# An attention and mixture-of-experts kernel: input loads three chunks ahead instead of four, the first chunks in halves, and three groups of small VectorE work in another order

## The chip, the cores and the metric

The kernel runs on one NeuronCore of a Trainium2 chip. The metric is the time of one execution on the device in microseconds (us), median of several runs.

## The reference

A linear attention with decay runs over 4 batches, 8 heads, 768 positions and 64 features; its output is laid out as 3072 tokens of 512 features. A gate with noise picks two of eight experts for each token, and the token goes through both experts' two-layer networks.

```python
state = gamma[None, :, None, None] * state + np.einsum('bhd,bhe->bhde', k[:, :, t], v[:, :, t])
y[:, :, t] = scale * np.einsum('bhd,bhde->bhe', q[:, :, t], state)
...
logits = x @ w_gate
noise_scale = np.log1p(np.exp(x @ w_noise))
noisy_logits = logits + noise_scale * noise
top2 = np.argpartition(-noisy_logits, 2, axis=1)[:, :2]
...
h = np.maximum(x[mask] @ w1[e], 0.0)
out[mask] += top2_w[mask, k, None] * (h @ w2[e])
```

## The kernel before

The order of instructions on every engine is written out by hand. The 3072 tokens are 24 chunks of 128 (`NCH`), six chunks (`NC`) to a batch.

**First stage, chunks.** `step(j)` for j = 0 to 22, and `step(23)` inside the first matmuls of expert 0. In program order, step j does this: TensorE (PE) makes the scores of chunk j+1 (`qk`, L354: q and k of chunk j+1 must have landed), turns the output of chunk j-1 (`x_turn`, L405), reads the state (`y_state`, L371). GpSimd (POOL) scales v of chunk j+1 (`v_scale`, L335, output vp); VectorE (DVE) masks the scores of chunk j+1 (`masked`, L359, two instructions, output am). The scores have two PSUM buffers for the two halves of a chunk, so `qk` of step j+1 needs `masked` of step j. ScalarE (ACT) and DVE finish chunk j-1 (`x_square`, `x_scale`, `x_split`). The SyncE queue (SPq) issues `load(j + AHEAD)` and then `x_store(j - 2)`, which waits for POOL's `x_low` (L437). PE ends the chunk with `y_mm` (L378 and, except in the last chunk of a batch, L388), which needs vp and am.

**Loads.** `load(j)` brings q and k of a chunk (in_qk, 512 KB) and v and k of the same chunk in rows (in_vk, 512 KB). Each has `AHEAD + 1` buffers, so the load in step j writes the buffers that chunk j-1 has left, with `AHEAD` at 4 or at 3. All inputs, the weights of expert 0 (`w_load`, in steps 2 to 5 for w1 and 14 to 17 for w2), the stores of x, and the transposes below are issued by the one SPq in program order; where one of them waits, all behind it wait.

**Small work.** Behind `y_mm` and `x_low` a step runs lists in the order `late`, `mid`, `todo`, `first_todo`. `P(j, ...)` puts into `mid`, `at(j, ...)` into `todo`, `at0` into `first_todo`. They hold the routing of the first batches (`route_*`), the token lists of expert 0 (`own_a`, `own_h`, `own_t`, `own_m`, `own_s`, `slots`) and the low halves of w1 (`w_lo_half(0, "1", i)`, L245: 512 columns; odd i are columns 512 to 1023, which the filter groups f = 4 to 7 of the first matmul read). `own_h` (L585) compares 128 lane numbers for each of 12 chunks, two chunks in step 15 and ten in step 16; `own_t` (L593, L595) is two short instructions behind it; `own_m` (L602, PE) of step 17 needs both.

**Into expert 0.** With the list, POOL gathers three blocks of tokens (`gather`, L743, in steps 17, 18 and 19, tile xg), and SPq transposes them into xe (`x_t`, L761, in the `mid` lists of steps 19, 20 and 21). `first(0)` to `first(7)` are the first matmuls over these 384 tokens (L888 to L890, tile pH); `first(0)` needs all three transposed blocks, and `first(4)` in its first four-matmul group k = 0 reads w1's low half 1 (the third matmul, L890) and in k = 3 half 7. `step(23)` runs between the halves of `first(0)`. From there on expert 0's rest and seven more experts follow.

Of the kernel before, what the change touches and what calls it, by code (L numbers as in the profile page):

```python
# [60 lines left out]
SOON = _C["vtab"][1]  # L61
# [43 lines left out]
def moe_kernel(ctx, tc, qk_rows, vk_rows, noise, wgn, w1, w2, ctab, qtab, xbuf, out):  # L105
    nc = tc.nc
# [30 lines left out]
    ct = consts.tile([128, CW - SOON], F32, name="ct")  # L137
# [3 lines left out]
    def K(n):  # L141
        a, b = _C[n]
        return cs[:, a:b] if b <= SOON else ct[:, a - SOON:b - SOON]
# [3 lines left out]
    trib = consts.tile([128, 128], BF, name="trib")  # L147
# [6 lines left out]
    tokn = consts.tile([128, NCH], F16, name="tokn")  # L154
# [4 lines left out]
    lanes = consts.tile([128, 128], F16, name="lanes")  # L159
    blks = consts.tile([128, NCOL], F16, name="blks")  # L160
# [64 lines left out]
    def w_parts(which, i):  # L225
        if which == "1":
            return WT["1h"][:, i, :], WT["1l"][:, i, :]
        return [WT["2" + n][:, 2 * i:2 * i + 2, :].rearrange("p a d -> p (a d)") for n in "hl"]
# [12 lines left out]
    def w_lo_half(e, which, i):  # L241
        st, ss, sc = ST[which, e]
        hi, lo = w_parts(which, i // 2)
        r = slice(i % 2 * 512, i % 2 * 512 + 512)
        nc.vector.scalar_tensor_tensor(lo[:, r], st[:, i * 512:(i + 1) * 512], sc[:, 0:1], hi[:, r],  # L245
                                       op0=OP.mult, op1=OP.subtract)
# [12 lines left out]
    loads = lctx.enter_context(tc.tile_pool(name="loads", bufs=3))  # L259
    IN = {}  # L260

    AHEAD = 4

    def load(j, pairs=("qk", "vk")):
        for n in pairs:
            t = loads.tile([128, 2, DM], F32, name="in_" + n, bufs=AHEAD + 1)
            src = {"qk": qk_rows, "vk": vk_rows}[n][j]
            if n == "vk" and j == 0:
                for i in range(2):
                    nc.sync.dma_start(t[:, i], src[:, i * DM:(i + 1) * DM])  # L270
            else:
                nc.sync.dma_start(t.rearrange("p a c -> p (a c)"), src)
            if n == "qk":
                IN["q", j], IN["k", j] = [t[:, i].rearrange("p (a c) -> p a c", a=HP) for i in range(2)]
            else:
                IN["v", j], IN["kt", j] = t[:, 0], t[:, 1]

    gq = loads.tile([128, NC, HP * C], F32, name="gq", bufs=1)
    for r in (slice(0, 2 * C), slice(2 * C, 4 * C)):
        nc.scalar.activation(gq[:, 0, r], gp[:, r], AF.Copy)  # L280
    load(0, ("qk",))
    nc.sync.dma_start(cs, ctab[:, :SOON])
    load(1, ("qk",))
    load(0, ("vk",))
    nc.sync.dma_start(wgf, wgn)
    load(2, ("qk",))
    load(1, ("vk",))
    for j in range(3, AHEAD):
        load(j, ("qk",))
        load(j - 1, ("vk",))  # L290
    load(AHEAD - 1, ("vk",))

# [45 lines left out]
    def q_table(c):  # L338

        for i in range(HP):  # L340
            nc.scalar.activation(gq[:, c, i * C:(i + 1) * C], gq[:, 0, i * C:(i + 1) * C], AF.Copy,
                                 scale=gt[:, c * HP + i:c * HP + i + 1])
# [385 lines left out]
    def at(j, f, *a):  # L728
        todo.setdefault(j, []).append((f, a))
# [40 lines left out]
    def P(j, f, *a, d=mid):  # L770
        d.setdefault(j, []).append((f, a))
# [13 lines left out]
    P(15, route_d, 0)  # L785
    P(15, own_a, 0)
    P(15, route_g, 0, nc.gpsimd)
    P(15, own_h, 0, 0, 2)
    at(16, gates_out, 0)
    P(16, own_h, 0, 2, 12)  # L790
    P(16, own_t, 0)
    P(16, route_e, 0)
    P(17, own_m, 0, 0, 2 * NC, d=late)
    P(17, own_s, 0)
    P(17, slots, 0, 3)
# [22 lines left out]
        if i < 3:  # L818
            at0((18, 20, 22)[i], w_sum, 0, "2", i)
    first_todo[9].insert(0, (w_scale, (0, "1")))  # L820
    for i, j in ((0, 10), (2, 11), (4, 12), (6, 14), (1, 18), (3, 21), (5, 23)):
        P(j, w_lo_half, 0, "1", i)
    at(3, nc.sync.dma_start, nz.rearrange("p c e -> p (c e)"), noise)
    at(4, nc.sync.dma_start, ct, ctab[:, SOON:])
    at(9, nc.vector.tensor_copy, trib, K("tri"))
    at(9, nc.vector.tensor_copy, lanes, K("lanes"))
    at(9, nc.vector.tensor_copy, blks, K("blks"))
    at(9, nc.vector.tensor_copy, tokn, K("tokn"))
    at(3, nc.vector.memset, grow, 0.0)
    at(4, nc.vector.memset, gatew, 0.0)  # L830
    at(9, nc.sync.dma_start, xbuf[:128, :DM], zero)
# [9 lines left out]
    def step(j):  # L841
# [14 lines left out]
        if j < NC - 3:  # L856
            q_table(j + 3)
        if j + AHEAD < NCH:
            load(j + AHEAD)
        if j > 1:  # L860
# [35 lines left out]
    def h_lo(p, f, n0, n1):  # L896
        nc.vector.scalar_tensor_tensor(hl[:, f, n0:n1], p, 0.0, hh[:, f, n0:n1], op0=OP.max, op1=OP.subtract)  # L897
# [115 lines left out]
    j = NCH - 1  # L1013
# [36 lines left out]
    w_hi(0, "2", 1)  # L1050
    h_lo(*p0)
    w_lo_half(0, "1", 7)
    h_lo(*p1)
    h_lo(*p2)
    h_hi(*p3)
# [58 lines left out]
    for e in range(E):  # L1114
# [4 lines left out]
        n, more = 0, e + 1 < E  # L1119
# [187 lines left out]
```

## Time and profile before

| | |
|---|---|
| time, median of 3 runs | 642.57 us (641.34 to 642.76) |
| the profiled execution | 644.79 us |
| its span, first to last instruction | 643.0 us |
| PE busy | 625.2 us (97%) |
| DVE, ACT, POOL busy | 291.1, 302.7, 203.6 us |
| mean granted TensorE clock | 0.997 of full speed |
| `qk` of step 1 starts, `qk` of step 14 starts | 11.63 us, 65.09 us |
| `qk`, 16 matmuls, when not held | 1.16 us |

PE's busy time is the span but for 18 us, so the question for any edit is which of PE's idle pieces it touches. An edit ahead of the point from which PE never waits moves all that follows by what it saves or costs there. A matmul group that is held up in its middle counts as busy, so a group that is longer than usual is a wait too.

### The profile page before, as it was taken

How to read it: one execution, taken by the hardware profiler on the slowest of the kernel's cores; microseconds unless marked ns; L12 is line 12 of the kernel's file. 1: busy time of each engine (PE TensorE's matmuls, PEld its weight loads, DVE VectorE, ACT ScalarE, POOL GpSimd, SP SyncE). 2: the span in 40 equal slices, each digit the busy share in tenths (PEclk: the TensorE clock that was granted, in tenths of full speed). 3: DMA queues.
4: the chain of work that ended last, by engine and by line, in shares of the span. 5: the costliest groups of instructions: out<-in, count | busy, mean ns of one | idle time of the engine just before them, and what ended most of it. 6: DMA issues, size and time to landing. Idle time of an engine off the chain costs nothing.

```text
span 643.0 us, 12833 instructions
## 1 busy us (share of the span) xinstructions
PE 625.2 (97%) x5223; PEld 379.2 (59%) x5223; DVE 291.1 (45%) x736; ACT 302.7 (47%) x582; POOL 203.6 (32%) x169
## 2 busy tenths in 40 slices
PE   8998989999999999999999999999999999999995
PEld 5887877559578545554455445544554465455574
DVE  4667997997454221654262226222622262215020
ACT  5778557615652443554354344434543454344121
POOL 2555556032540143104320533043303420430214
PEclk9999999999999999999999999999999999999998
DMA  8999997998769067736673567557744764472303
GB/s 304 407 407 407 325 368 139 335 243 294 163 106 303 10 123 131 234 84 110 123 212 131 102 130 199 143 88 129 202 151 84 134 197 148 91 140 35 49 9 44
DMA packets 87656, 113.04 MB, mean 176 GB/s; under 512 B 59910, under 2 KB 61068, under 8 KB 84012
## 3 DMA queue, kind: packets, MB, share of 16 engines
q1 hardware_dynamic: 75808, 85.56, 43.4%
q0 software_dynamic: 11776, 26.63, 22.5%
q8 instruction: 42, 0.69, 0.4%
q14 instruction: 18, 0.15, 0.1%
q10 hardware_dynamic: 12, 0.01, 0.0%
HBM read 72.66 MB, written 26.42 MB: 154 GB/s over the span
## 4 chain that ended last, share of the span: by engine, by line
PE 90%; DVE 3%; DMA 2%; issue 2%; POOL 1%; ACT 1%; SPq 0%; POOLq 0%; ACTq 0%; DVEq 0%
PE pH L888 13%; PE pH L890 13%; PE pH L889 13%; PE pO L934 12%; PE pO L936 12%; PE pO L935 12%; PE pY L378 3%; PE pA L354 3%; PE pT L405 2%; PE pT L990 2%; PE pO L978 2%; PE pY L371 1%; DMA xbuf<-x 1%; PE pU L388 1%; DMA in_vk<-vk 1%
## 5 line engine op out<-in xcount | busy, mean ns | idle before, releaser
L925 POOL DMA_INDIRECT out<-ot,idx x51 | 84.4, 1654 | 320.4 <-ACT ot L920 191.7
L888 PE MATMUL pH<-xe,w1h 128*128 128x384 f16 (+5 forms) x576 | 180.9, 314 | 1.1 <-DVE ga L539 1.1
L890 PE MATMUL pH<-xe,w1l 128*128 128x384 f16 (+5 forms) x576 | 180.9, 314 | 0.0
L889 PE MATMUL pH<-xe,w1h 128*128 128x384 f16 (+5 forms) x576 | 180.8, 314 | 0.0
L897 DVE SCALAR_TENSOR_TENSOR hl<-pH,hh 128x384 f16<-128x384 f32 (+5 forms) x144 | 75.6, 527 | 140.1 <-ACT hh L894 139.4
L936 PE MATMUL pO<-w2h,hl 128*128 128x512 f16 x344 | 130.4, 379 | 0.0
L935 PE MATMUL pO<-w2l,hh 128*128 128x512 f16 x344 | 130.4, 379 | 0.0
L934 PE MATMUL pO<-w2h,hh 128*128 128x512 f16 x344 | 130.4, 379 | 0.0
L894 ACT ACTIVATE hh<-pH 128x384 f16<-128x384 f32 (+5 forms) x144 | 67.1, 467 | 122.9 <-PE pH L890 112.0
L920 ACT ACTIVATE ot<-pO,gse 128x512 f32<-128x512 f32 x45 | 30.9, 687 | 155.2 <-PE pO L936 142.9
L238 DVE SCALAR_TENSOR_TENSOR w1l<-wst,wsc,w1h 128x1024 f16<-128x1024 f32 x28 | 35.9, 1283 | 97.6 <-ACT w1h L233 97.6
L888 PEld LDWEIGHTS <-w1h 128*128 128x128 f16 x576 | 56.3, 98 | 34.2 <-issue 3.9
L890 PEld LDWEIGHTS <-w1l 128*128 128x128 f16 x576 | 56.3, 98 | 31.0
L889 PEld LDWEIGHTS <-w1h 128*128 128x128 f16 x576 | 56.3, 98 | 29.7
L210 ACT ACTIVATE junk<-wst 128x1024 bf16<-128x1024 f32 x64 | 67.2, 1050 | 0.0
L743 POOL DMA_INDIRECT xg<-xbuf,idx x54 | 55.3, 1025 | 29.3 <-issue 12.4
L936 PEld LDWEIGHTS <-hl 128*128 128x128 f16 x344 | 33.6, 98 | 40.6
L934 PEld LDWEIGHTS <-hh 128*128 128x128 f16 x344 | 33.6, 98 | 40.6 <-issue 0.4
L935 PEld LDWEIGHTS <-hh 128*128 128x128 f16 x344 | 33.6, 98 | 39.6
L437 POOL TENSOR_TENSOR x<-x,x 128x512 f16<-128x512 f32 x23 | 27.4, 1190 | 41.2 <-ACT x L436 19.3
L233 ACT ACTIVATE w2h<-wst,wsc 128x1024 f16<-128x1024 f32 x32 | 36.5, 1139 | 0.8 <-DVE wsc L188 0.8
L233 ACT ACTIVATE w1h<-wst,wsc 128x1024 f16<-128x1024 f32 x32 | 36.2, 1137 | 0.0
(185 smaller groups left out, 660.0 us busy)
## 6 DMA issues: line engine op xcount, KB each, us to landing
wst<-w SPq DMA_DIRECT2D x28, 1024.0 KB, 7.8
in_qk<-qk SPq DMA_DIRECT2D x24, 512.0 KB, 7.9
in_vk<-vk SPq DMA_DIRECT2D x23, 512.0 KB, 8.7
xbuf<-x SPq DMA_DIRECT2D x24, 256.0 KB, 7.2
out<-zero SPq DMA_DIRECT2D x6, 1024.0 KB, 8.8
wst<-w SPq DMA_DIRECT2D x8, 512.0 KB, 7.4
xg<-xbuf,idx POOLq DMA_INDIRECT x54, 4.7
xe<-xg SPq DMA_TRANSPOSE x54, 4.5
```

The lines of the kernel that those rows point to most:

```text
L210: nc.scalar.activation(junk, st[:, i * 1024:(i + 1) * 1024], AF.Square, accum_out=ss[:, i:i + 1])
L233: nc.scalar.activation(hi, st[:, i * 1024:(i + 1) * 1024], AF.Copy, scale=sc[:, 0:1])
L743: nc.gpsimd.indirect_dma_start(out=x[:n], out_offset=None, in_=xbuf[:128 + B0 * S] if e == 0 and t < 3 else xbuf, in_offset=bass.IndirectO ...
L888: nc.tensor.matmul(p[:, :n], whi, xh, start=(k == 0), stop=False)
L889: nc.tensor.matmul(p[:, :n], whi, xl, start=False, stop=False)
L890: nc.tensor.matmul(p[:, :n], wlo, xh, start=False, stop=(k == KT - 1))
L894: nc.scalar.activation(hh[:, f, n0:n1], p, AF.Relu)
L897: nc.vector.scalar_tensor_tensor(hl[:, f, n0:n1], p, 0.0, hh[:, f, n0:n1], op0=OP.max, op1=OP.subtract)
L925: nc.gpsimd.indirect_dma_start(out=out, out_offset=bass.IndirectOffsetOnAxis(ap=idx[:n, i:i + 1], axis=0), in_=ot[:n], in_offset=None, com ...
L934: nc.tensor.matmul(p, a, WT["2h"][:, f, :], start=(f == 0), stop=False)
L935: nc.tensor.matmul(p, a, WT["2l"][:, f, :], start=False, stop=False)
L936: nc.tensor.matmul(p, c, WT["2h"][:, f, :], start=False, stop=(f == FT - 1))
```

## The change

- `AHEAD` is 3: the start issues chunks 0 to 2, `load(3)` is in step 0, and each later load is issued one step later than before; the buffers are four in place of five.
- Chunks 0 and 1 are loaded in halves of 256 KB (`APART`), four transfers each; before, only in_vk of chunk 0 was.
- `own_h` runs as one instruction over all 12 chunks in step 16, behind `own_t`; `route_e` of the first batches moves to step 17.
- w1's low half 1 moves from step 18 to behind half 7, between the `h_lo` of `first(0)` and of `first(1)`.
- The table `ct` is loaded in step 1, not 4, and its four copies run in step 6, not 9.

```diff
-    AHEAD = 4
+    AHEAD = 3
+
+    APART = 2
...
-            if n == "vk" and j == 0:
+            if j < APART:
                 for i in range(2):
                     nc.sync.dma_start(t[:, i], src[:, i * DM:(i + 1) * DM])
...
     nc.sync.dma_start(wgf, wgn)
-    load(2, ("qk",))
-    load(1, ("vk",))
-    for j in range(3, AHEAD):
+    for j in range(2, AHEAD):
         load(j, ("qk",))
         load(j - 1, ("vk",))
     load(AHEAD - 1, ("vk",))
...
     P(15, route_g, 0, nc.gpsimd)
-    P(15, own_h, 0, 0, 2)
     at(16, gates_out, 0)
-    P(16, own_h, 0, 2, 12)
     P(16, own_t, 0)
-    P(16, route_e, 0)
+    P(16, own_h, 0, 0, 12)
+    P(17, route_e, 0)
...
-    for i, j in ((0, 10), (2, 11), (4, 12), (6, 14), (1, 18), (3, 21), (5, 23)):
+    for i, j in ((0, 10), (2, 11), (4, 12), (6, 14), (3, 21), (5, 23)):
         P(j, w_lo_half, 0, "1", i)
     at(3, nc.sync.dma_start, nz.rearrange("p c e -> p (c e)"), noise)
-    at(4, nc.sync.dma_start, ct, ctab[:, SOON:])
-    at(9, nc.vector.tensor_copy, trib, K("tri"))
-    at(9, nc.vector.tensor_copy, lanes, K("lanes"))
-    at(9, nc.vector.tensor_copy, blks, K("blks"))
-    at(9, nc.vector.tensor_copy, tokn, K("tokn"))
+    at(1, nc.sync.dma_start, ct, ctab[:, SOON:])
+    at(6, nc.vector.tensor_copy, trib, K("tri"))
+    at(6, nc.vector.tensor_copy, lanes, K("lanes"))
+    at(6, nc.vector.tensor_copy, blks, K("blks"))
+    at(6, nc.vector.tensor_copy, tokn, K("tokn"))
...
     w_lo_half(0, "1", 7)
+    w_lo_half(0, "1", 1)
     h_lo(*p1)
```

## Rows read from the trace of the kernel before

**Rows 1.** Windows: stretch, its us, each engine's busy us (instructions), clock, DMA share, GB/s.

```profile
10.14:66.00 55.86, 53.57 (x1121) 47.76 (x1121) 39.07 (x117) 41.35 (x102) 28.45 (x26) 1.00 1.03 406
66.00:106.70 40.70, 36.10 (x806) 31.70 (x802) 35.91 (x121) 23.76 (x63) 24.49 (x23) 1.00 1.03 306
...
128.00:636.00 508.00, 507.83 (x3060) 283.86 (x3058) 195.83 (x420) 217.59 (x374) 144.11 (x107) 1.00 0.59 137
```

**Rows 2.** Timeline, the start: start, us, engine, line, operation, tiles, [idle before, releaser].

```profile
2.87 0.91 SPq L270 DMA_DIRECT2D in_vk<-vk  x2
...
9.05 1.04 POOL L335 TENSOR_TENSOR vp<-in_vk,cs 128x512 f32<-128x512 f32 x1 [7.98 <-DMA in_vk<-vk]
...
10.14 1.09 PE L378 MATMUL pY<-am,vp 128*64 128x128 f32 x16 [0.66 <-POOL vp L335]
```

**Rows 3.** DMA issues (count, KB each, median us to landing) at 0, 3 and 6 us.

```profile
in_qk<-qk SPq DMA_DIRECT2D x1, 512.0 KB, 3.6
...
in_vk<-vk SPq DMA_DIRECT2D x2, 256.0 KB, 6.1
...
in_qk<-qk SPq DMA_DIRECT2D x2, 512.0 KB, 9.8
```

**Rows 4.** Waits of PE up to 128 us: total us, times, longest.

```profile
PE pY L371 <- issue: 2.0, 3, 1.1
...
PE pT L405 <- issue: 1.1, 1, 1.1
```

**Rows 5.** Timeline, the token list's work in steps 16 and 17.

```profile
78.62 1.48 DVE L585 TENSOR_TENSOR a<-lanes,lf 128x1280 f16<-128x1280 f16 x1
...
79.76 1.35 POOL L437 TENSOR_TENSOR x<-x,x 128x512 f16<-128x512 f32 x1 [1.19 <-ACT x L436]
...
80.02 1.19 DVE L593 TENSOR_TENSOR ob<-blks,lf 128x84 f16<-128x84 f16 x1
...
82.40 1.28 DVE L359 TENSOR_TENSOR am<-pA,mask 128x512 f32<-128x512 f32 x2
...
83.13 1.75 PE L354 MATMUL pA<-in_qk 64*128 64x128 f32 x16
```

**Rows 6.** Timeline, w1's low half 1 and what follows it.

```profile
87.29 3.39 DVE L245 SCALAR_TENSOR_TENSOR w1l<-wst,wsc,w1h 128x512 f16<-128x512 f32 x1
...
88.97 1.15 POOL L437 TENSOR_TENSOR x<-x,x 128x512 f16<-128x512 f32 x1
...
92.05 1.75 PE L354 MATMUL pA<-in_qk 64*128 64x128 f32 x16 [0.93 <-DVE am L359]
...
94.92 0.78 PE L405 MATMUL pT<-turn,yt 64*64 64x80 f32 x32 [1.11 <-ACT x L431]
```

**Rows 7.** Timeline, the last loads, a gather, the transposes, the first expert matmul.

```profile
87.06 0.39 SPq L272 DMA_DIRECT2D in_qk<-qk  x1
...
94.55 1.35 SPq L761 DMA_TRANSPOSE xe<-xg  x1
...
97.10 0.98 POOL L743 DMA_INDIRECT xg<-xbuf,idx  x1
...
102.08 1.23 SPq L761 DMA_TRANSPOSE xe<-xg  x1
...
106.73 0.32 PE L888 MATMUL pH<-xe,w1h 128*128 128x384 f16 x1 [1.07 <-DVE ga L539]
```

**Rows 8.** DMA issues around 87 us (a load, the first gather) and 97 us (third gather).

```profile
in_qk<-qk SPq DMA_DIRECT2D x1, 512.0 KB, 8.6
xg<-xbuf,idx POOLq DMA_INDIRECT x1, 7.8
...
xg<-xbuf,idx POOLq DMA_INDIRECT x1, 5.0
```

**Rows 9.** Timeline, w1's low half 7 and the first L890 matmul of `first(4)`.

```profile
118.28 0.74 DVE L245 SCALAR_TENSOR_TENSOR w1l<-wst,wsc,w1h 128x512 f16<-128x512 f32 x1
...
119.27 0.33 PE L890 MATMUL pH<-xe,w1l 128*128 128x384 f16 x1
```

## The prediction

> **What bounds the kernel now.** I read the windows first [rows 1]. From 128 to 636 us PE is busy 507.83 of 508.00 us: nothing there can be hurried except by starting it earlier. The idle time that an edit can reach lies before: 55.86 - 53.57 = 2.3 us in the first-stage steps up to 66 us, 40.70 - 36.10 = 4.6 us between 66 us and the first expert matmul, and the wait for the first inputs. So the question is when that first expert matmul, at 106.73 us [rows 7], starts in the changed kernel, and what is lost just behind it. Then I read the timelines of these places for the releaser of each pause, and the DMA issues for how long a transfer takes when SPq is full.
>
> Three things are to be seen. First, the start: PE's first pY waits for vp, and vp for the first in_vk half [rows 2]. Second, VectorE: short instructions with two inputs in SBUF last long exactly while POOL is busy, L593 until POOL's L437 ends, and w1's low half 1 for 3.39 us where the same form takes 0.74 [rows 5, 6, 9]. What follows is late masking, so PE's scores wait or take 1.75 us instead of 1.16. Third, one queue: SPq sits in front of the first transpose until its gather has landed (L761 starts at 94.55, the gather takes 7.8, so it was issued at some 86.8) [rows 7, 8].
>
> **Part 1, the halves at the start.** Two more issues (the second halves of q/k of chunks 0 and 1) stand ahead of v's first half: 2 x 0.91/2 = 0.9 us later [rows 2] if its landing time stays 6.1 us [rows 3]. Against that, what is issued behind it and shares the DMA engines with it also starts 0.9 us or more later. A transfer twice its size landed in 3.6 us with nothing else in flight and in 9.8 us in a full queue [rows 3], so landing goes by what is in flight. The bounds are therefore 0.9 us later and 0.9 - (6.1 - 3.6) = 1.6 us earlier. I take 0.4 us earlier, near the middle of the two: 6.1 lies between 3.6 and 9.8, so the company is already half of what it can be, and it comes later. PE is packed behind pY, so this passes through. **-0.4 (+0.9 to -1.6).** The row here shows 256 KB in 6.1 us beside other transfers and 512 KB in 3.6 us alone, that is, size hardly counts against company. The Trainium skill (DMA: Bandwidth & Descriptors, Rules for kernel authors and Anatomy of one DMA) speaks against the halves: it wants transfers of at least 1 MiB and gives about 2.0 us fixed plus bytes over 436 GB/s for each, on another issuing path, so by it a 512 KB load in two halves that do not overlap would cost 5.2 us instead of 3.2. By that rule part 1 would be a loss; it is the start of the second rival below.
>
> **Part 2, three chunks ahead, up to 66 us.** Steps are (65.09 - 11.63)/13 = 4.1 us. A load is issued about when chunk j-1's buffer is left, so q and k have some two steps, 8 us, in place of three. In the full queue they take 9.8 us [rows 3], which would be 1.8 us late; but one chunk less in flight is 1.05 MB, 2.6 us at 406 GB/s [rows 1], so 7.2 us, and on time by 0.8. I take no wait, bound 1.8 us. A gain is possible in PE's pauses that wait for nothing shown: 2.0 + 1.1 us, four pieces, each in the middle of a run of equal matmuls [rows 4], while the DMA share is 1.03 [rows 1]. What they wait for is not shown; that they come with full DMA queues is why I count a little. **-0.5 (+1.8 to -2.5).** The table load in step 1 and its four copies in step 6 cost nothing: one small transfer among the 22 MB that move by 66 us (406 GB/s x 55 us), and VectorE has 55.86 - 39.07 = 16.8 us free there [rows 1]; without that cover they would cost four short casts, under 1 us.
>
> **Part 3, own_t ahead of own_h.** Now ten chunks of comparison take 1.48 us, own_t starts behind them at 80.02, in the moment POOL works on x_low (79.76 to 81.11), and masking begins at 82.40 [rows 5]. Turned round, own_t starts at about 78.6, before POOL's x_low, and twelve chunks take 1.48 x 12/10 = 1.8 us; masking begins some 1.2 to 1.6 us earlier. PE can use of it only what its scores were held: 1.75 - 1.16 = 0.6 us [rows 5]. The price is that own_h keeps POOL's x_low waiting up to 1 us; POOL idles 1.19 us ahead of it, so it is covered. route_e, two tiny instructions, goes behind own_m's issue and delays the list, which the first gather does not wait for. **-0.6 (0 to -0.9).**
>
> **Part 4, w1's low half 1 leaves step 18.** It occupies VectorE from 87.29 to 90.68, while POOL runs gather, vp and x_low without a break to 90.12 [rows 6]; the 0.74 us of work starts only then. What hangs behind it: the routing sum, then masking, so PE's scores wait 0.93 us and are stretched by 1.75 - 1.16 = 0.59, and ACT's chain, so x_turn waits 1.11 us [rows 6]. Sum **-2.6 us (0 to -2.6)** at this place. The rows show a held instruction that runs when POOL stops. The Trainium skill (SBUF — State Buffer, SBUF: two separate sides) names it: a VectorE instruction with two SBUF inputs and a GpSimd instruction exclude each other for whole instructions. The trace agrees (3.39 against 0.74 us).
>
> At the new place POOL has nothing to do, so 0.74 us is its length, but VectorE ends half 7 at 119.02 and now half 1 at 119.7, and PE reads half 1 at 119.27 [rows 9]: PE waits 0.4 us, and the list work of the next batches, behind it on VectorE and waited for by PE a little later, makes it up to 0.7. **+0.6 (0 to +0.8).**
>
> **Part 5, the last load passes the transposes.** With 3 ahead, load(23) is in step 20, not 19: behind the first x_t in SPq's order. So it can't be issued until the first gather has landed. Parts 3 and 4 bring that gather forward by some 1 us, from 86.8: it lands at 85.8 + 7.8 = 93.6, the transpose takes SPq 1.35 us [rows 7, 8], and q/k of chunk 23 are issued at about 94.9. They land 3.6 to 8.6 us later [rows 3, 8]; no other load is in flight then, so I take 5.5: 100.4 us. PE would be ready for them at 106.7 - 1.07 (its wait there) - 3.2 (parts 3 and 4) - 4.1 (a step) = 98.3 us. So PE waits 2 us (0.2 to 5.2), and expert 0 could start at 104.5. The other thing that it needs, the third transpose: its gather at 97.10 moves up with the chain by 3.2 us to 93.9, lands after 5.0 to 7.8 us, and the first matmul came 4.65 us after the transpose's issue (102.08 to 106.73) [rows 7, 8]: 103.6 to 106.3. I take 104.9 for the later of both. The gain of parts 3 to 5 up to there is 106.7 - 104.9 = **-1.8 us**, where the path without this queue would give 1.07 + 3.2 = -4.3.
>
> **Sum.** -0.4 - 0.5 - 1.8 + 0.6 = -2.1 us. On the profiled execution, 644.79, that is 642.7; it lies 2.2 us over the median of the runs, so the forecast for the median is 642.57 - 2.1 = **640.5 us**.
>
> **Rivals.** *The queue takes it all (slower).* Where: PE's L354 of step 22, waiting for in_qk of chunk 23. If the gather doesn't come earlier and the load takes 8.6 us, it is issued at 94.55 + 1.35 = 95.9, lands at 104.5, and the first expert matmul starts at 108.6, 1.9 us later than now. With +0.6 behind and nothing won at the start: +2.5, 645.1 us. It decides at a landing of about 102.9 (107.0 less a step): beyond it the kernel is slower. For it: full queues up to 100 us; against: it is the last load, with nothing behind it.
>
> *Nothing that can be measured.* The halves cost their 0.9 us (the page's direction, priced by rows), the third transpose stays late at 106.0 or the loads are 1 us late in the early steps: +0.9 - 0.5 - 0.7 + 0.6 = +0.3, to -0.8; 642.0 to 642.9.
>
> *All of it comes.* Load and transpose are in time, expert 0 starts at 102.9, PE's unexplained pauses halve: -0.4 - 1.5 - 3.8 + 0.4 = -5.3, 637.3 us.
>
> **How the numbers follow.** Chances: forecast 0.54, nothing 0.20, all 0.12, slower 0.14. The time is the forecast's, 640.5. The range leaves out the far ends of the best and the slower case: 638.0 to 643.4; the forecast's own range by its bounds is 638.5 to 642.3. About 0.2%, 1.3 us, is what a measurement of this kernel can tell from no change. Faster by more: all of the best, most of the forecast, 0.61. Within: the nothing case and the edge of the forecast, 0.25. Slower: 0.14.
>
> **What would show it.** VectorE's L245 at 87 us gone, the two waits behind it gone (part 4 right; if PE's scores of step 20 still wait for masking, another instruction took its place). L593 at 0.2 to 0.3 us. A wait of L354 for in_qk near 98 us, with SPq's load behind L761 (part 5); none, and the first expert matmul under 104 us, would prove it too dear. L890 waiting for VectorE near the first third matmul of first(4). The first vp before 9.05 us. Waits for in_qk before 66 us would prove part 2 wrong.

## The result, and the profile of the changed kernel

| | before | after |
|---|---|---|
| time, median | 642.25 us (641.34 to 642.76) | 648.45 us (647.25 to 649.32) |
| ratio, 95% interval | | 1.0097 [1.0075, 1.0118] |
| profiled execution, its span | 644.79, 643.0 us | 649.32, 646.9 us |
| mean granted clock | 0.997 | 0.995 |

The change makes the kernel 6.2 us slower. The forecast was 640.5 us; the time lies above its range and above the rival that was slower.

First the windows, with the columns of [rows 1]: stretch, its us, busy us of PE, PEld, DVE, ACT and POOL (instructions), clock, DMA share, GB/s.

```profile
10.14:66.00 55.86, 52.03 (x1109) 46.52 (x1107) 39.28 (x111) 40.96 (x101) 28.26 (x26) 1.00 1.01 383
66.00:109.90 43.90, 37.59 (x816) 33.41 (x815) 31.94 (x118) 23.52 (x62) 24.99 (x23) 0.96 1.01 312
128.00:636.00 508.00, 507.58 (x3056) 282.66 (x3055) 198.91 (x432) 218.05 (x375) 142.26 (x106) 1.00 0.59 139
...
104.13:109.90 5.77, 5.53 (x103) 4.89 (x104) 2.24 (x6) 1.67 (x5) 1.04 (x1) 0.70 0.87 250
```

From 128 us on nothing has changed against [rows 1]. PE's idle time up to 66 us is 3.8 us where it was 2.3, the DMA engines bring 383 GB/s where they brought 406, and the stretch to the first expert matmul is 3.2 us longer, its last 5.8 us at a granted clock of 0.70. The waits of PE up to 128 us (total us, times, longest) and the timeline of PE (start, us, engine, line, operation, tiles, [idle before, releaser]) name the places:

```profile
PE pA L354 <- DMA in_qk<-qk: 5.2, 3, 3.7
...
PE pH L889 <- DVE w1l L245: 0.3, 1, 0.3
```

```profile
35.77 1.16 PE L354 MATMUL pA<-in_qk 64*128 64x128 f32 x16 [1.05 <-DMA in_qk<-qk]
...
91.49 1.16 PE L354 MATMUL pA<-in_qk 64*128 64x128 f32 x16 [0.41 <-DMA in_qk<-qk]
...
99.76 0.64 PE L388 MATMUL pU<-vp,in_vk 128*64 128x64 f32 x16
104.13 1.23 PE L354 MATMUL pA<-in_qk 64*128 64x128 f32 x16 [3.74 <-DMA in_qk<-qk]
105.29 1.34 PE L405 MATMUL pT<-turn,yt 64*64 64x80 f32 x32
...
109.91 0.32 PE L887 MATMUL pH<-xe,w1h 128*128 128x384 f16 x1 [0.24 <-issue]
```

Three waits for q and k have come, one near 36 us, one near 91, one of 3.74 us at step 22. Behind the long one a turn of 32 matmuls takes 1.34 us instead of 0.78. The first expert matmul starts at 109.91 us, not 106.73 [rows 7]. The timeline of the SP queue shows what the long wait hangs on:

```profile
87.36 0.33 SPq L274 DMA_DIRECT2D in_vk<-vk  x1
89.88 0.33 SPq L448 DMA_DIRECT2D xbuf<-x  x1
94.06 1.36 SPq L761 DMA_TRANSPOSE xe<-xg  x1
95.52 0.58 SPq L274 DMA_DIRECT2D in_qk<-qk  x1
```

The first gather is issued at 85.88, the transpose that waits for it at 94.06, and chunk 23's q and k behind it at 95.52. PE goes on at 104.13, 8.6 us after that issue. VectorE and POOL in the same stretch, and at the new place of w1's low half:

```profile
78.96 0.28 DVE L593 TENSOR_TENSOR ob<-blks,lf 128x84 f16<-128x84 f16 x1
...
79.43 1.75 DVE L585 TENSOR_TENSOR a<-lanes,lf 128x1536 f16<-128x1536 f16 x1
81.10 1.28 DVE L359 TENSOR_TENSOR am<-pA,mask 128x512 f32<-128x512 f32 x2
...
88.27 1.28 DVE L359 TENSOR_TENSOR am<-pA,mask 128x512 f32<-128x512 f32 x2
...
121.47 1.41 DVE L245 SCALAR_TENSOR_TENSOR w1l<-wst,wsc,w1h 128x512 f16<-128x512 f32 x2
```

L593 takes 0.28 us, not 1.19 [rows 5]; the 3.39 us piece at 87 us is gone [rows 6]; at its new place it and half 7 take 1.41 us together. So the small work did here what it should.

**A second look at the kernel before.** The same kernel, profiled again (run 642.46 us, span 640.7), starts its first expert matmul 2.5 us earlier than in [rows 7], almost without a wait:

```profile
99.32 0.63 PE L387 MATMUL pU<-vp,in_vk 128*64 128x64 f32 x16
99.89 1.16 PE L353 MATMUL pA<-in_qk 64*128 64x128 f32 x16
...
104.24 0.32 PE L887 MATMUL pH<-xe,w1h 128*128 128x384 f16 x1 [0.28 <-DVE yt L381]
```

Against this execution the loss can be followed without a remainder. Up to the end of chunk 22's last matmuls after is 0.45 us late (100.40 against 99.95): its pY began 0.48 us later and it waited 1.46 us for q and k, and it won back 1.5 us in between. From there to the first expert matmul it takes 9.51 us against 4.29: 3.74 us of wait, 1.48 us of slower work at the lower clock. Together 5.67 us. From the first expert matmul to the end of the span it is 537.0 us against 536.5. The sum, 6.2 us, is the difference of the two spans. That the medians differ by as much is chance: the measured time is longer than the span, by 2.35 to 2.42 us in every run of the changed kernel and by 1.75 to 1.89 us in before, so 0.6 us of the loss lies outside the span, and what is inside is nearer 5.6.

That last figure holds for the other kernels too: the rest of the span was 536.3 to 536.5 us in before (both executions) and in every kernel with w1's half at its old place, 537.0 to 537.5 where it stands at its new place, and more, 538.2 to 539.9, only in three profiles whose clock was low just behind it. So inside the span an edit is worth what it does to the start of the first expert matmul, plus 0.65 us for w1's move.

### The profile page after: what moved, and what is told of

Its sections match the earlier page's. It is cut to its first block, busy times and chain, and to the rows that moved or that the text cites. A ratio compares the mean times of both kernels' runs of the same rounds, so it can differ in the third digit from the quotient of the medians.

```text
span 646.9 us, 12838 instructions
## 1 busy us (share of the span) xinstructions
PE 627.7 (97%) x5223; PEld 381.5 (59%) x5223; DVE 287.5 (44%) x735; ACT 302.8 (47%) x582; POOL 204.7 (32%) x169
## 4 chain that ended last, share of the span: by engine, by line
PE 89%; DMA 6%; DVE 2%; issue 1%; ACT 1%; POOL 1%; POOLq 0%; SPq 0%; ACTq 0%; DVEq 0%
PE pH L887 13%; PE pH L889 13%; PE pH L888 13%; PE pO L933 12%; PE pO L934 11%; PE pO L935 11%; DMA in_qk<-qk 4%; PE pA L354 3%; PE pY L378 2%; PE pT L405 2%; PE pT L989 2%; PE pO L977 2%; PE pY L371 1%; DMA in_vk<-vk 1%; PE pU L388 1%
```

## The experiments

Theories, named before the runs: *the queue place* (A): the last load behind the transposes is the whole loss; *bytes* (D): the DMA engines have work up to the first expert matmul, so that bytes not moved early with three chunks ahead are missing at the end, wherever the wait shows; *the clock* (K): a pause ahead of the first expert matmul costs a second time through a lower clock. Ratios are to the kernel before on the same chip, with the 95% interval. "List order" is the new order of the token list's work (`own_t`, `own_h`, `route_e`); the earlier load and copies of the table `ct` were not run alone. "mm1" is the start of the first expert matmul in the profiled execution.

| kernel | ratio | median, us | mm1, us |
|---|---|---|---|
| before + 3 ahead | 1.0077 [1.0049, 1.0105] | 647.24 | 108.64 |
| after with 4 ahead | 1.0014 [0.9998, 1.0031] | 644.21 | 106.65 |
| before + w1's move | 0.9977 [0.9960, 0.9993] | 642.22 | 105.71 |
| the same again | 0.9982 [0.9963, 1.0001] | 642.41 | 103.10 |
| before + list order | 0.9998 [0.9981, 1.0014] | 643.22 | 105.99 |
| before + halves | 1.0012 [0.9999, 1.0026] | 643.5 | 105.28 |
| before + w1's move + list order | 1.0041 [1.0025, 1.0057] | 644.93 | 105.05 |
| the same again | 0.9994 [0.9967, 1.0020] | 642.92 | 104.25 |
| after, chunk 23 ahead of the transposes | 1.0087 [1.0061, 1.0113] | 648.86 | 108.76 |
| after, half of w2 not loaded | 1.0053 [1.0036, 1.0071] | 647.15 | 108.01 |
| after, w2 loaded in steps 9 to 12 | 1.0072 [1.0047, 1.0097] | 647.52 | 108.00 |
| after, both: chunk 23 first, half of w2 not loaded | 1.0119 [1.0090, 1.0149] | 650.05 | 106.99 |
| before + w1's move, half of w2 not loaded | 0.9996 [0.9979, 1.0012] | 641.9 | 100.99 |
| after with 4 ahead, PE kept busy ahead of mm1 | 1.0059 [1.0038, 1.0079] | 646.82 | 108.54 |
| before, 3 ahead from step 10 on | 1.0038 [1.0015, 1.0060] | 644.06 | 105.78 |
| before, 3 ahead up to step 9 | 1.0016 [0.9993, 1.0039] | 643.08 | 106.60 |

A caution that the repeats taught: w1's move with the list order gave 1.0041 on one chip and 0.9994 on another, and the intervals do not meet. Differences of under half a per cent between kernels of different chips are hints below, no more. What is far beyond it is the gap between three and four chunks ahead: on one chip 1.0077 and 1.0087 stand against 1.0014 and 0.9977.

**Which part costs: three chunks ahead alone, and everything else.**

```diff
-    AHEAD = 4
+    AHEAD = 3
```

in the kernel before, and back to 4 in the changed one, on one chip.

> The kernel before with three chunks ahead alone. Theory A: carries the whole loss and more, since the old order of the small work is kept: PE waits for in_qk of chunk 23 less than 3.7 us, because it arrives later itself; 644 to 649. Rival B: within 0.2% of the kernel before, 641 to 643.5.

> The changed kernel with AHEAD back at 4; halves, table order and w1's low half 1 stay as changed. Theory A (the last load waits on SyncE's queue behind the first transpose, and PE then waits 3.7 us and runs 5.8 us at a granted clock of 0.70): both go, first expert matmul near 103 to 105 us instead of 109.9, time 639 to 642, at or below the kernel before. Rival B (the halves or the moved small work cost the time): stays above 645.

Measured: 1.0077 and 1.0014, and the whole change 1.0097. The loss is that of the loads. The other parts together give no gain: on this chip w1's move alone stands at 0.9977, so what comes with it (the halves, the list order, `ct`) takes back some 2.4 us, and which of them does is not shown. The expectation of 639 to 642 us with four ahead was missed. But the kernel with three ahead alone loses in another way than the whole. Its timeline of PE:

```profile
31.50 1.16 PE L352 MATMUL pA<-in_qk 64*128 64x128 f32 x16 [0.36 <-DMA in_qk<-qk]
...
36.47 1.16 PE L352 MATMUL pA<-in_qk 64*128 64x128 f32 x16 [1.60 <-DMA in_qk<-qk]
...
103.94 1.16 PE L352 MATMUL pA<-in_qk 64*128 64x128 f32 x16
...
108.64 0.32 PE L886 MATMUL pH<-xe,w1h 128*128 128x384 f16 x1 [0.64 <-DVE cb L526]
```

Nearly 2 us go in waits for q and k by 37 us, and another 1.5 us near 97, where the granted clock is 0.63 from 96 to 100 us behind the two waits of [rows 6], which this kernel keeps (0.92 and 1.12 us): a turn of 32 matmuls takes 1.34 us there, not 0.78. The same two waits in before left the clock at 1.00 [rows 1]. At step 22 the load is in time, because PE itself comes late. The changed kernel comes there earlier, and waits there instead.

**The queue place.** In the changed kernel chunk 23 is loaded in step 19, ahead of the first transpose.

```diff
+        if t == 0:
+            P(19, load, NCH - 1)
...
-        if j + AHEAD < NCH:
+        if j + AHEAD < NCH - 1:
```

> The changed kernel with one thing moved: the load of chunk 23 is issued in step 19 just ahead of the first transpose, not in step 20 behind it. Theory A (the place in the queue): it is issued when chunk 19's buffers are free, near 91.5 us instead of 95.5; the wait of 3.7 us shrinks to 0 to 1 us and the clock stays at 1.00; 641 to 645. Rival C (one chunk less ahead is late wherever it is issued, since a load takes 8 us): the wait stays at 2 us or more, 646 to 648.

Measured 1.0087: nothing was won. The load is issued at 90.47 us and the wait for q and k is gone; in its place PE stops in the middle of a run of matmuls whose inputs are there (its timeline, then its windows):

```profile
100.57 0.48 PE L354 MATMUL pA<-in_qk 64*128 64x128 f32 x2
103.31 1.55 PE L354 MATMUL pA<-in_qk 64*128 64x128 f32 x14 [2.25 <-issue]
...
108.76 0.34 PE L889 MATMUL pH<-xe,w1h 128*128 128x384 f16 x1
```

```profile
104.00:108.00 4.00, 4.00 (x77) 3.43 (x75) 1.59 (x4) 1.45 (x4) 0.10 (x1) 0.58 1.23 197
```

Such pauses for nothing shown sum to 8.4 us here, 3.2 in each of the two executions of before, and 1.4 to 6.5 in the others, with three ahead and with four. A falls as the whole cause: the place in the queue decides where the time is lost, not that it is lost.

**Bytes.** Half of expert 0's w2 is not loaded (four short POOL instructions fill its place with a constant, so that part of the output is left out), 1.05 MB less, with the changed kernel and with w1's move alone; and, with nothing left out, w2 loaded five steps earlier.

```diff
-        at(14 + i, w_load, 0, "2", i)
+        at(7 + i, w_fill, i)
+        at(14 + i, w_load_half, i)
```

```diff
-        at(14 + i, w_load, 0, "2", i)
+        at(9 + i, w_load, 0, "2", i)
```

> The changed kernel with half of expert 0's w2 not loaded in steps 14 to 17 (four transfers of 256 KB in place of 512; the other columns are set to a constant in steps 7 to 10, so this part of the output is left out). SyncE's order is untouched. Theory D (the DMA engines have some 37.5 MB to move before the first expert matmul, are full all the way, and with three chunks ahead they are 1.1 MB behind from 66 us on): 1.05 MB less gives about 3 us back, the wait for chunk 23 falls under 1.5 us, the clock stays at 1.00, time 642 to 645.5. Theory A (only the place behind the transpose counts): the wait stays at 3 us or more, 647 to 649.

> The kernel before with w1's low half 1 moved, and half of expert 0's w2 not loaded in steps 14 to 17 (the rest set to a constant in steps 7 to 10; that part of the output is left out). Theory D (bytes decide up to the first expert matmul): 1.05 MB less than in the kernel with w1's move alone gives another 1.5 to 3 us, time 638.5 to 640.5, first expert matmul at 102.5 to 104. If PE and the small engines decide: like w1's move alone, 641 to 642.

> The changed kernel with expert 0's w2 loaded in steps 9 to 12 instead of 14 to 17, when with three chunks ahead the DMA engines move 330 to 355 GB/s and not 408. Theory D: the bytes that are late are moved in that spare time, PE's wait for chunk 23 shrinks below 1.5 us, time 642 to 645.5. Theory A: 647 to 649. If the loads of steps 9 to 12 now wait behind w2, a wait for in_qk between 50 and 70 us shows it.

Measured: 1.0053, 0.9996 and 1.0072. Without the bytes the changed kernel wins 2.8 of its 6.2 us by the ratios, across two chips, but its two waits stay (timeline of PE of the changed kernel without the bytes), against what D expects:

```profile
35.64 1.16 PE L364 MATMUL pA<-in_qk 64*128 64x128 f32 x16 [1.00 <-DMA in_qk<-qk]
...
102.01 1.16 PE L364 MATMUL pA<-in_qk 64*128 64x128 f32 x16 [2.91 <-DMA in_qk<-qk]
...
108.01 0.32 PE L898 MATMUL pH<-xe,w1h 128*128 128x384 f16 x1 [1.94 <-DVE ga L549]
```

With four chunks ahead the bytes are worth nothing in the median (641.9 us), though one execution started its experts at 100.99. Loaded earlier, in the changed kernel, they bring 1.6 us by the ratio, within the intervals' reach of nothing; the sign that its expectation named came, a wait of 0.89 us for q and k at 60.80 us, and the wait for chunk 23 was 2.50 us, not under 1.5.

**Both at once.**

> The changed kernel with both remedies at once: chunk 23 loaded ahead of the first transpose, and half of expert 0's w2 not loaded (that part of the output is left out). Alone the first gave nothing and the second about 2.8 us. If each was held by the other (a queue place and too many bytes in series): 641.5 to 644, no wait of PE over 1.5 us near 100 us. If the bytes alone count: 645 to 647, as with half of w2 alone.

Measured 1.0119, the slowest of all. PE is at the first expert matmul by 104.0 us and then waits 3.03 us for the transposed blocks, and the granted clock is 0.50 from 108 to 112 us. So the two remedies do not add up, and an earlier arrival was lost again.

**Where three ahead costs: from step 10 on, or up to step 9.**

```diff
+        for n in ([j + 4] if j < 10 else [] if j == 10 else [j + 3]):
...
+        for n in ([j + 3] if j < 10 else [13, 14] if j == 10 else [j + 4]):
```

> The kernel before, four ahead in steps 0 to 9, no load in step 10, three ahead from step 11 on (five buffers kept). If three chunks ahead cost late (1 MB of bytes missing from 66 us on and the last load at the transposes): 645.5 to 648, no wait for in_qk before 60 us. If they cost in the first steps: 642 to 644.

> The kernel before, three ahead in steps 0 to 9, two loads in step 10, four ahead from then on. If the cost is early (in_qk waits of 1 to 2 us near 35 us in every kernel with three ahead): 644 to 646 with these waits in its trace, and the time isn't made good later. If the missing bytes can be caught up while the DMA engines move under 360 GB/s and only the late part costs: 642 to 643.5.

Measured on one chip: 1.0038 and 1.0016, and 1.0119 for one execution of the changed kernel there (649.65 us to 641.99). The late part costs something; of the early part the ratio does not show it, since its interval holds 1. 644.06 us for the late part is in neither of its expected ranges. Both kernels keep five buffers, so what four buffers cost by themselves is not separated. The timelines of PE, of the late part and then of the early one:

```profile
95.36 1.16 PE L354 MATMUL pA<-in_qk 64*128 64x128 f32 x16 [1.21 <-DVE i L487]
...
100.09 1.16 PE L354 MATMUL pA<-in_qk 64*128 64x128 f32 x16 [0.63 <-DMA in_qk<-qk]
...
105.78 0.32 PE L889 MATMUL pH<-xe,w1h 128*128 128x384 f16 x1 [1.62 <-DMA xe<-xg]
```

```profile
36.60 1.36 PE L351 MATMUL pA<-in_qk 64*128 64x128 f32 x16 [1.96 <-DMA in_qk<-qk]
```

PE waits near 36 us, ahead of chunk 8's scores, in all eight profiles with three ahead in the first steps and in none of the twelve with four there: 1.0 to 2.0 us for q and k in five, 0.35 to 0.89 us in three where the profile names VectorE instructions that the scores do not read. (In one of the three, chunk 23 ahead of the transposes, q and k landed at 34.79 us and PE went on at 34.92.) In the late part PE stops for 1.21 us at chunk 22's scores, where a VectorE instruction is named that they do not read either, and for 0.63 us at chunk 23's.

**The clock.** The changed kernel with four ahead takes 3.21 us of pause ahead of its first expert matmul, since PE arrives at 103.4 while the third transpose is issued at 102.12, as in [rows 7]. Its profiled execution took 648.55 us, 4.3 above its median. Its timeline of PE and its windows:

```profile
102.81 0.63 PE L388 MATMUL pU<-vp,in_vk 128*64 128x64 f32 x16
106.65 0.48 PE L887 MATMUL pH<-xe,w1h 128*128 128x384 f16 x1 [3.21 <-DVE ga L540]
```

```profile
108.00:112.00 4.00, 4.00 (x39) 2.90 (x39) 0.31 (x2) 0.87 (x4) 0.00 (x0) 0.50 0.25 74
112.00:116.00 4.00, 4.00 (x60) 2.83 (x57) 2.22 (x6) 3.21 (x8) 1.16 (x1) 0.87 0.16 59
```

0.50 of full speed is the lower of the two levels, 1.2 GHz. The remedy tried: fifteen matmuls on constants in the pause.

```diff
+    busy(15)
```

> The changed kernel with AHEAD at 4 and fifteen matmuls of constants (about 3.2 us) on PE ahead of first(0), where that kernel's PE idles 3.2 us waiting for the transposed blocks and then runs at a granted clock of 0.50 for some 6 us. Theory K (the pause costs again through the clock): PE's clock stays at 1.00, the first expert matmul starts at the same 106.5 to 107.5 us, second-layer matmuls start near 127.5 us instead of 130.6, time 640.5 to 642.5 against 644.2. If the clock is not what costs: 644 or more.

Measured 1.0059, slower than without. The clock stayed up (0.998 over the execution), but second-layer matmuls start at 129.78 us, not near 127.5: the constants took 3.45 us, from 105.25 to 108.5 in the profile, and where the pause is shorter they stand in the way. K is right on the price of a pause in single executions, 1.5 us in the changed kernel and as much with three ahead alone. As the cause of the loss it is unlikely: the pauses come first, and with four ahead the median hardly suffers from them. The constants were not tried in the changed kernel itself.

**The other parts, one by one.** w1's move, the list order and the halves, each in the kernel before:

```diff
-    for i, j in ((0, 10), (2, 11), (4, 12), (6, 14), (1, 18), (3, 21), (5, 23)):
+    for i, j in ((0, 10), (2, 11), (4, 12), (6, 14), (3, 21), (5, 23)):
...
+    w_lo_half(0, "1", 1)
```

```diff
-    P(15, own_h, 0, 0, 2)
...
-    P(16, own_h, 0, 2, 12)
...
+    P(16, own_h, 0, 0, 12)
+    P(17, route_e, 0)
```

```diff
-            if n == "vk" and j == 0:
+            if j < 2:
```

> The kernel before with w1's low half 1 moved alone. By the forecast's part 4: 2.6 us less ahead of the third transpose, which then ends the wait, and 0.4 to 0.7 us lost behind at the first L890 of first(4): first expert matmul 103 to 105.5, time 639.5 to 642. If the gather's landing decides instead: same as before, 641.5 to 643.

> The kernel before with the token list's order alone (own_t ahead of one own_h, route_e in step 17). By the forecast's part 3: masking in step 17 some 1.2 us earlier, PE gains 0.6 us there, then waits as much longer for the third transpose: 641.5 to 643.5, within 0.2% of the kernel before. If POOL is held up by the longer own_h: up to 1 us slower.

> The kernel before with chunks 0 and 1 loaded in halves alone (four ahead as before). By the changed kernel's trace the first vp starts near 8.75 us instead of 9.05, 0.3 us earlier. If the DMA engines set the time up to the first expert matmul, this gain is lost again there: 642 to 643.5, within 0.2% of the kernel before. If PE sets it: 0.3 us faster, which can't be told from that; slower by more than 1 us would say that more and smaller transfers cost something later.

> The kernel before with w1's low half 1 moved and the token list's new order, four ahead, no halves: the two parts that were not slower alone. If both gains add up: 1.5 + 0 to 0.6 us, 640.5 to 641.5. If the transposed blocks or the DMA engines are the limit behind them: no better than w1's move alone, 641 to 642; if PE then pauses long enough for its clock to fall, as with four ahead and all other parts: 643 to 645.

Two repeats on another chip, the move alone and with the list order:

> The kernel before with w1's low half 1 moved alone, a second time, on the same chip as the next run. If the gain of the first series (ratio 0.9977, interval 0.9960 to 0.9993) is the move's, the ratio comes out between 0.996 and 0.999 again; if it was the chance of one chip and one series, at 0.999 to 1.002.

> The kernel before with w1's move and the order of the tables, a second time. If the order of the tables costs some 3 us beside the moved half (first series 1.0041, interval 1.0025 to 1.0057, though alone it gave 0.9998), the ratio is 1.003 to 1.006 here and 0.005 above the other run of this call; if the difference lay between two chips, both runs agree within 0.0025.

Measured: w1's move gives 1.2 to 1.5 us on two chips (the second interval ends at 1.0001); it is the only version with an interval below 1. List order and halves alone give nothing that can be told from zero. The 1.0041 of move and list order together did not come again. (The 8.75 us for vp in the expectation of the halves is not that of the changed kernel's trace, which has 8.34.)

Two second executions, of the changed kernel and of before, were taken to see how far one profile can be trusted:

> The changed kernel once more, for a second profiled execution. If the wait of 3.7 us for chunk 23 belongs to the program, it is there again with 2.5 us or more, and the granted clock falls behind it; if it was chance, it is under 1.5 us and the time is lost elsewhere.

> The kernel before once more, for a second profiled execution: how far PE's pauses without a shown releaser (3.3 us in the first one) and the first expert matmul (106.73 us) differ from one execution to the next. If the pauses come from how full the DMA engines happen to be, 2 to 5 us; if they belong to the program, 3.3 us at the same places.

The changed kernel again took 649.65 us, but its long wait at step 22 was 1.28 us, not 3.74 (timeline of PE):

```profile
103.01 1.26 PE L353 MATMUL pA<-in_qk 64*128 64x128 f32 x16 [1.28 <-DMA in_qk<-qk]
...
108.98 0.32 PE L886 MATMUL pH<-xe,w1h 128*128 128x384 f16 x1 [1.80 <-DVE ga L538]
```

The total is the same, the places are not: the rest stands in the wait of 1.80 us for the transposed blocks and in longer pauses for nothing shown (6.5 us in sum, not 4.6). In before those pauses sum to 3.2 us both times, at four of the same five matmuls.

## Why the prediction was wrong, step by step

**Part 2 failed, by its landing time and its lead.** It took no wait, with q and k landing in 7.2 us in a queue that holds one chunk less, against a lead of two steps, 8 us. In the changed kernel chunk 8's q and k are issued at 27.68 us, PE is ready for them at 34.72 and goes on at 35.77: a lead of 7.0 us, and 8.1 us from issue to use. The queue was not shorter there. By the sizes of what is issued up to 30 us and the bytes moved by then, after has 2.3 MB on the way and before 1.6 (with three ahead in the first steps 2.3 to 2.7 in all eight profiles, 1.4 to 2.2 in the twelve others); w1's third and fourth piece are now issued 2 and 3 us earlier than they were. From `qk` of step 1 to that of step 14 PE takes 52.9 to 55.5 us in the eight profiles (mean 54.2) and 50.9 to 53.6 in the eleven with four ahead throughout (mean 52.5): a loss of 1.7 us, where the term was -0.5. The pauses from which its gain was to come sum to 4.6 and 6.5 us in the changed kernel's two executions, not to less than 3.2.

The DMA engines deliver less as well, but later. The windows of before and of after:

```profile
30.00:66.00 36.00, 33.95 (x691) 29.90 (x691) 25.51 (x83) 28.75 (x67) 18.18 (x17) 1.00 1.03 404
40.00:50.00 10.00, 8.79 (x197) 7.62 (x201) 6.99 (x35) 8.39 (x19) 5.11 (x5) 1.00 1.03 409
50.00:60.00 10.00, 9.82 (x219) 8.62 (x212) 6.97 (x15) 7.57 (x17) 6.14 (x6) 1.00 1.04 407
```

```profile
30.00:66.00 36.00, 32.49 (x682) 28.77 (x681) 24.76 (x77) 28.65 (x68) 18.28 (x17) 1.00 1.00 380
40.00:50.00 10.00, 9.56 (x209) 8.54 (x207) 7.09 (x34) 8.11 (x20) 4.33 (x4) 1.00 1.02 405
50.00:60.00 10.00, 10.00 (x238) 9.00 (x234) 7.78 (x20) 8.83 (x19) 6.38 (x6) 1.00 0.98 354
```

From 30 to 66 us the ten other profiles with four ahead throughout give 404 to 407 GB/s, the eight with three ahead in the first steps 370 to 389, and the kernel that goes from four to three in step 10 gives 388. The two groups do not touch. The difference opens at 50 us: by then after has moved all but 0.2 of the 18.5 MB issued, while before still has 1.4 MB on the way, so the engines are short of work rather than slower. Up to 66 us it is 380 GB/s against 361: 66 x 0.380 = 25.1 MB against 23.8. Of the 1.3 MB that are missing, 1.05 MB are the chunk itself, asked for a step later. At 306 to 312 GB/s, which both kernels move from there to the first expert matmul, 1.3 MB are some 4 us that have to be found before it. That this deficit is the cause of the late loss fits the kernel without the bytes (2.8 us won), not the two waits that it kept, nor the run with both remedies; it is borne out in part, and not shown.

**Part 5 failed by its terms.** The load's issue was forecast for 94.9 us and came at 95.52. Its landing was taken as 5.5 us and was 8.6, the upper bound. "No other load is in flight then" was wrong where it counted: the second load of the same chunk and the stores, gathers and transposes that had been issued kept the DMA share at 1.29 from 96 to 100 us. PE was ready at 100.39 us, not at 98.3. So of the 5.4 us from the 104.5 forecast for this path to 109.91, the issue is 0.6, the landing 3.1, the slower clock 1.5. The rival "the queue takes it all" had the place (L354 of step 22), the price (8.6 us) and the order of things; its first expert matmul was 108.6 us, and without the slower clock after's would have started at 109.91 - 1.48 = 108.4. It had 0.14. But the run with the load ahead of the transposes shows that even this rival named a place rather than the cause: take the place away, and the time goes elsewhere.

**What no step priced.** The pause of 3.74 us was followed by 5.77 us at a granted clock of 0.70, which cost another 1.48 us. The prediction read the clock of [rows 1], 1.00, and took it as given for the changed kernel. Nor did it price the 0.6 us outside the span. (In the rival that sees nothing measurable, +0.3 to -0.8 is 642.9 to 641.8 us, not to 642.0.)

**The baseline failed.** The sum was made against one execution, with 106.73 us for the first expert matmul. That execution lay 2.2 us over the median, which the prediction said and then subtracted as if it lay outside the argument. It lay inside: the second execution starts its experts at 104.24, with a wait of 0.28 us in place of 1.07, and w1's low half 1 held for 2.28 us rather than 3.39. So the forecast of 104.9 for the changed kernel was, against a usual execution, no gain at all.

**Part 4 was right, at both places.** The piece at 87 us, late masking and the two waits behind it [rows 6] are gone, and the price behind the first expert matmul, forecast +0.6, is 0.65. Its gain of 2.6 us was sized on the slow execution and overlaps with part 3: with the list order alone the half at its old place takes 0.74 us, since it no longer meets POOL. Measured net: -1.2 to -1.5 in two series of the move alone. That a VectorE instruction with two SBUF inputs and a POOL instruction exclude each other agrees with the Trainium skill (SBUF — State Buffer, SBUF: two separate sides) here too: 0.7 us each at the new place, where POOL is idle.

**Part 3 was right in mechanism**: L593 at 0.28 us and masking at 81.10, not 82.40 [rows 5]. Its price came too: POOL's x_low beside `own_h` takes 2.11 us, not 1.35. Alone the part gives no time, 0.9998.

**Part 1 gave no gain that shows.** In the changed kernel vp began at 8.34 us, before 9.05, and pY 0.3 us earlier, as forecast. But over all profiles vp begins at 7.77 to 8.98 us in the nine with halves and at 7.99 to 9.05 us in the eleven without, so the sign named for this part proves nothing, and the 0.3 us were luck. By the Trainium skill (DMA: Bandwidth & Descriptors, Rules for kernel authors and Anatomy of one DMA), which wants 1 MiB and more in a transfer and gives each about 2.0 us that do not depend on its size, an estimate for halves that do not overlap is a loss of some 2 us; the halves alone measured 1.0012 [0.9999, 1.0026], 1.7 us at most.

**The pauses for nothing shown** come at the same instructions in every kernel (three matmuls into L371 near 81 us; two into an L354 near 100), while the DMA share is near 1.0, with 0.2 to 2.3 us each. The traces say what they go with. The page of before has an instruction queue, q8, with 42 transfers of 16 KB. The twenty profiles have 103 pauses of 0.3 us or more. All stand at one of twelve places in the order of matmuls, 125 to 127 matmuls from one to the next, and each ends 1.3 to 1.7 us after the end of one such transfer, the longest 2.0 us after. That longest one, 2.25 us with chunk 23 ahead of the transposes, follows a transfer that takes 4.13 us, from 97.14 us on, where the others up to 106 us take 0.9 to 2.0. Its share of the 16 DMA engines in 1 us is four times that of the transfer before it (DMA views of that kernel, 91.5 to 92.5 us and 97 to 98 us):

```profile
q8 instruction: 1, 0.02, 6.5%
...
q8 instruction: 1, 0.02, 25.8%
```

So PE most likely waits there for its own instructions, which share the full DMA engines with the loads. No run took these transfers away, so it is borne out by the times alone.

**What stays open.** How the late loss is shared between the queue, the bytes and these pauses. Since kernels with four ahead have the pauses too, they are not by themselves what three ahead costs.

## What to carry to other kernels

A prefetch depth is not only a distance in time: one chunk less asked for leaves the DMA engines short of work as soon as the queue has been emptied (here from 50 us on), and its bytes come due later, here most likely at the first place behind which nothing can be hidden. A landing time read in a full queue should not be shortened by a chunk before it is known what moves into its place. Before a sum is made against one profiled execution, a pause of a microsecond in it should be seen twice, for it may belong to the execution and not to the kernel. And compute that is made faster ahead of a stage that waits for transfers arrives early, waits longer, and can pay for the pause a second time in clock.

## What the runs showed of the hardware

- The granted clock fell behind pauses of PE of 2.25 us (0.58 of full speed from 104 to 108 us), 3.03 and 3.21 us (0.50 from 108 to 112) and 3.74 us (0.70 over 5.8 us), but also behind one of 1.96 us (with three ahead up to step 9: 0.68 from 36 to 40 us, 0.50 from 40 to 44) and behind two of about 1 us each (with three ahead alone: 0.63 from 96 to 100 us). It stayed at 1.00 behind the same two in before, and behind 2.91 and then 1.94 us in the changed kernel without half of w2. So the length of one pause did not settle it in these runs.
- A gather issued earlier into full queues did not help: with four ahead and the other changes the third gather was issued 5.4 us earlier than in [rows 7], and landed 10.4 us later where it had taken 5.0, so the third transpose was issued at 102.12 against 102.08.
- A DMA share of 0.98 in place of 1.04 from 50 to 60 us went with 354 GB/s in place of 407: a busy share near 1 does not say that the queues are full.
- PE's pauses without a releaser ended 1.3 to 2.0 us after the end of a 16 KB transfer of the instruction queue in all 103 cases of 0.3 us or more.
